# Mish as four nested products instead of five, in a fused attention and dense kernel whose softmax is shared by two engines

## The chip, the cores and the metric

The kernel runs on one core of a Trainium2 chip. A core has a matrix engine (TensorE, in the profile PE for matmuls and PEld for weight loads), a vector engine (VectorE, DVE), an engine for activation functions (ScalarE, ACT), a general one (GpSimd, POOL), and a queue that issues most transfers (SyncE, SP). They run at the same time and wait for each other by semaphores. The metric is the time of one execution on the device in microseconds, as the median of several runs; lower is better. Before the change it is 871.78 us (three runs, 871.4 to 873.9).

## The reference

Two branches over the same x (2048 tokens, 640 features, bf16), mixed by a gate per token. Branch A is attention with 32 heads of 20 dimensions; branch B is a dense layer to 1536 features, the Mish activation, and a dense layer back.

```python
qkv = (x @ wqkv).reshape(B, S, 3, H, Dh)            # H = 32, Dh = 20
scores = einsum("bhqd,bhkd->bhqk", q, k) * Dh ** -0.5
a = (softmax(scores) @ v) @ wo                      # heads put together first
h = x @ w1 + b1
sp = log1p(exp(-abs(h))) + where(h > 0, h, 0)       # softplus
b = (h * tanh(sp)) @ w2                             # Mish of h, then w2
g = sigmoid((x * gate_w).sum(-1, keepdims=True))
out = g * a + (1 - g) * b
```

## The kernel before

The kernel is written as a plan: Python code walks through the program in the order in which it should run, keeps an estimated clock for each engine, and appends each operation to its engine's list. The order on every engine is thus fixed when the kernel is built, and it depends on the planner's costs, due times and limits.

The backbone is the softmax. Its 2048 score tiles (128 keys by 512 queries, by head and block; the last block in two halves) are worked off in 683 slots of three tiles. In each slot TensorE makes three score tiles in one half of six PSUM banks (`emit_s`, L1062), ScalarE exponentiates them in one instruction into the tile ETS (`emit_e`, L1084), and TensorE multiplies the result with V (`pv`, L1198). Two slots of scores are in flight, five slots of ETS.

In some slots one tile, a "unit", is taken off ScalarE. ScalarE then exponentiates two tiles (1024 columns), and VectorE makes the exponential of the third from the bits of the number: one instruction that evicts the scores from PSUM with a scale and an offset (L1112), and three of 512 columns that correct it with a polynomial (two of L1128, one of L1130; `emit_x`). Two such chains, with the tiles EM and ER, run interleaved. `choose` decides for each slot whether it gives off a unit: only if a buffer is free, if VectorE's backlog is under BEHIND, and if a unit's chain (estimated by CHAIN) ends before its head group does. Before that, the condition in the main loop (L1519) allows no unit where tasks are late by LAG slots and the backlog is over SPARE, or where `room` finds that the VectorE work still owed (MISH per hidden task among it) does not fit the slots that are left.

Between slots TensorE is given tasks from a list by due time: the projections for Q, K and V, packed into shared tiles and moved through DRAM (QS, KS) by SP; the hidden layer `h_task` (L851, eviction with bias on VectorE, L861), the output of branch B `b_task` (L911, eviction times 1 - g in `OMG`, L918), and the output projection `p_task` (L935, mixing in L941). Matmuls without use (L1472, and repeated scores) fill TensorE's idle time. After each head group VectorE copies the accumulated output out (L1276) and divides it by the row sums, which go through three small transfers on SP's queue (RR, SUMS, BCT; L1279 to L1289).

The part that is changed belongs to branch B. Two `h_task`s fill 1024 columns of HB. Then `mish` appends one ScalarE instruction, a tanh of half the (shifted) h into the tile U, in W2R or REG (L884), and a chain of VectorE instructions of 1024 columns (L900 to L904), which leave the activation in HB. They wait in the lane `blend`, from which `work` picks them when VectorE's planned time has a hole. There are 24 such groups. The activation is left without its constant factor, which stands in `OMG` (L759) and is multiplied in with the gate. A test of the inputs' size (`flag_ops`, `flag_end`) must end before the first hidden task; it chooses between this program and a slower one that is not run here.

## Time and profile before

| | |
|---|---|
| median of three runs | 871.78 us (871.4 to 873.9) |
| the profiled execution | 871.46 us, of it the span 869.6 us |
| PE busy | 756.0 us (87%), 6350 matmuls |
| DVE busy | 827.8 us (95%), 1306 instructions |
| ACT busy | 852.5 us (98%), 714 instructions |
| transfers | 48.42 MB, 56 GB/s on average |
| exponentials (L1084) | 683, 833.9 us busy |
| tanh (L884) | 18 to REG, 23.0 us; 6 to W2R, 7.1 us |
| third-tile evictions (L1112) | 77 + 70 + 33 + 25 + 11 = 216 |

The span is what the profiler saw from the first instruction to the last; the execution's own time has some 2 us around it. Busy times are those of the recorded intervals. Records of neighbouring instructions on one engine overlap a little, so the mean duration of a record is longer than the step from one start to the next. A row of a group reads: line, engine, operation, tile written <- tiles read, shape, count, then busy time and mean ns of one, then the idle time of the engine before them and who ended it.

### The profile page before, as it was taken

The page shows a single profiled execution, that of the slowest core. Times are in us where ns is not written, and L with a number is a line of the kernel's source. Part 1 is how long each engine was busy: PE and PEld are TensorE (multiplying, and loading weights), DVE is VectorE, ACT ScalarE, POOL GpSimd, SP SyncE. Part 2 cuts the span into 40 slices and gives each one's busy share as a digit, 9 for nine tenths or more (in the row PEclk, how much of TensorE's full clock was granted, in tenths as well). Part 3 has the DMA queues.
Part 4 walks back from the last instruction along what each step waited for, and adds up shares of the span by engine and source line. Part 5 has one row for each costly group of instructions (what it writes and reads, how often), then busy time and mean ns, then how long its engine had stood idle before and what let it go on. Part 6 is the DMA issues. An engine that isn't in the chain of part 4 may idle for free.

```text
span 869.6 us, 15516 instructions
## 1 busy us (share of the span) xinstructions
PE 756.0 (87%) x6350; PEld 262.6 (30%) x6395; DVE 827.8 (95%) x1306; ACT 852.5 (98%) x714; POOL 7.3 (1%) x14
## 2 busy tenths in 40 slices
PE   7888888888889988899888898898888889889896
PEld 3333332233223332223223333232333233233232
DVE  5799999999999999999999999999999999999995
ACT  6999999999999999999999999999999999999996
POOL 2000000000000000000000000000000000000000
PEclk9999999999999999999999999999999999999998
DMA  9611310011233222302111121111212121010001
GB/s 223 86 60 40 108 40 24 11 59 49 76 90 99 64 59 71 122 16 49 32 44 44 59 60 47 47 32 56 60 43 69 48 60 52 8 29 26 18 14 35
DMA packets 76318, 48.42 MB, mean 56 GB/s; under 512 B 22104, under 2 KB 71888, under 8 KB 76192
## 3 DMA queue, kind: packets, MB, share of 16 engines
q1 hardware_dynamic: 73872, 46.86, 19.7%
q8 instruction: 53, 0.87, 0.4%
q10 hardware_dynamic: 2256, 0.47, 0.3%
q0 software_dynamic: 112, 0.01, 0.1%
q14 instruction: 25, 0.20, 0.1%
HBM read 37.64 MB, written 7.52 MB: 52 GB/s over the span
## 4 chain that ended last, share of the span: by engine, by line
ACT 93%; PE 3%; DVE 3%; DMA 1%; issue 0%; DVEq 0%; SPq 0%
ACT ETS L1084 90%; ACT REG L884 2%; PE PS L1062 1%; ACT W2R L884 1%; DMA OTN<-in_A_x_dram 1%; DMA RR<-OUNG 0%; PE PS L1198 0%; DVE ER L1128 0%; PE PS L607 0%; DVE EM L1128 0%; DVE HB L861 0%; PE PS L851 0%; PE PS L935 0%; PE PS L679 0%; DVE W2R L1112 0%
## 5 line engine op out<-in xcount | busy, mean ns | idle before, releaser
L1084 ACT ACTIVATE ETS<-PS 128x1536 bf16<-128x1536 f32 (+1 forms) x683 | 833.9, 1488 | 2.1 <-PE PS L1062 1.9
L1062 PE MATMUL PS<-QT,KT 32*128 32x512 bf16 (+1 forms) x2221 | 278.0, 378 | 93.8 <-ACT ETS L1084 78.9
L1198 PE MATMUL PS<-ETS,V_all 128*21 128x512 bf16 (+1 forms) x1888 | 211.7, 380 | 0.9 <-DVE OUNG L1276 0.4
L1062 PEld LDWEIGHTS PS<-QT,KT 32*128 32x128 bf16 x2221 | 69.1, 91 | 307.4 <-ACT ETS L1084 281.2
L1198 PEld LDWEIGHTS PS<-ETS,V_all 128*21 128x21 bf16 x1888 | 48.5, 89 | 95.2 <-issue 87.5
L911 PE MATMUL PS<-W2R,HB 128*128 128x320 bf16 x384 | 73.7, 302 | 0.3 <-DVE HB L861 0.2
L1128 DVE SCALAR_TENSOR_TENSOR ER<-ER 128x512 f32<-128x512 f32 x108 | 73.6, 681 | 0.1
L1128 DVE SCALAR_TENSOR_TENSOR EM<-EM 128x512 f32<-128x512 f32 x108 | 73.3, 679 | 0.1
L1112 DVE TENSOR_SCALAR REG<-PS 128x512 f32<-128x512 f32 x77 | 52.6, 685 | 3.9 <-PE PS L1062 2.5
L851 PE MATMUL PS<-XB,REG 128*128 128x256 bf16 x360 | 55.2, 275 | 0.7 <-DVE HB L861 0.5
L1112 DVE TENSOR_SCALAR XE<-PS 128x512 f32<-128x512 f32 x70 | 48.0, 686 | 5.3 <-PE PS L1062 4.4
L911 PEld LDWEIGHTS PS<-W2R,HB 128*128 128x128 bf16 x384 | 28.4, 97 | 38.6 <-issue 27.4
L1472 PE MATMUL PS<-KT 128*128 128x512 bf16 x120 | 36.5, 383 | 2.3 <-issue 1.7
L851 PEld LDWEIGHTS PS<-XB,REG 128*128 128x128 bf16 x360 | 27.9, 97 | 26.0 <-issue 23.9
L861 DVE TENSOR_TENSOR HB<-PS,B1T 128x512 bf16<-128x512 f32 x48 | 32.7, 682 | 0.3
L901 DVE SCALAR_TENSOR_TENSOR U<-U 128x1024 f32<-128x1024 f32 x24 | 29.1, 1213 | 0.0
L902 DVE SCALAR_TENSOR_TENSOR U<-U,HB 128x1024 f32<-128x1024 f32 x24 | 29.0, 1209 | 0.0
L1128 DVE SCALAR_TENSOR_TENSOR EM<-REG 128x512 f32<-128x512 uint16 x39 | 26.6, 683 | 0.3
L1130 DVE SCALAR_TENSOR_TENSOR REG<-EM,REG 128x512 int32<-128x512 f32 x39 | 26.5, 679 | 0.0
L1128 DVE SCALAR_TENSOR_TENSOR ER<-REG 128x512 f32<-128x512 uint16 x38 | 25.9, 683 | 0.2
L1130 DVE SCALAR_TENSOR_TENSOR REG<-ER,REG 128x512 int32<-128x512 f32 x38 | 25.8, 680 | 0.0
L935 PE MATMUL PS<-WOQ,QT 128*128 128x320 bf16 x128 | 25.1, 305 | 0.7 <-DVE HB L941 0.3
(136 smaller groups left out, 827.1 us busy)
## 6 DMA issues: line engine op xcount, KB each, us to landing
REG<-in_B_w_dram SPq DMA_DIRECT2D x36, 320.0 KB, 3.1
BCT<-SUMS SPq DMA_DIRECT2D x31, 256.0 KB
W2R<-in_B_w_dram SPq DMA_DIRECT2D x12, 320.0 KB, 3.2
KT<-KS SPq DMA_DIRECT2D x28, 128.0 KB
QT<-QS SPq DMA_DIRECT2D x112, 20.0 KB
QS<-WOQ SPq DMA_DIRECT2D x16, 128.0 KB, 2.1
KS<-OTN SPq DMA_DIRECT2D x16, 128.0 KB, 1.7
W2R<-in_B_w_dram SPq DMA_DIRECT2D x1, 1920.0 KB, 8.9
```

The costliest lines, as they stand in the source:

```text
L851: return lambda e, bank: e.matmul(PS[:, bank, i * HW:(i + 1) * HW], w1b(n1)[:, f, i * P:(i + 1) * P], xt(c)[:, f, cols], start=(f == 0), s ...
L861: ev = dve(lambda e: e.tensor_tensor(hb, PS[:, bank, :].rearrange("p (i t) -> p i t", i=2), bias, ALU.add), [last, b_load, *guarded, *b_re ...
L901: piece(two, lambda e: e.scalar_tensor_tensor(U2[:, :], U2[:, :], EVEN[0], U2[:, :], ALU.add, ALU.mult))
L902: piece(two, lambda e: e.scalar_tensor_tensor(U2[:, :], U2[:, :], EVEN[1], h, ALU.add, ALU.mult))
L911: return lambda e, bank: e.matmul(PS[:, bank, 0:HALF], HB[:, hc % 2, f, t * P:(t + 1) * P], W2[:, f, half * HALF:(half + 1) * HALF], start ...
L1062: op = pl.add("pe", lambda e, i=i, g=real(g), tile=tile, j=j, cols=cols, c=c, of_q=of_q: e.matmul(scores(s)[:, i, cols], KT[32 * j:32 * j ...
L1084: e_op[s] = pl.add("act", lambda e: e.activation(ETS[:, s % NETS, 0:n, :], scores(s)[:, 0:n, :], AF.Exp, scale=SCALE, bias=LIFT if fast el ...
L1112: ev_op[s] = dve(lambda e: e.tensor_scalar(y, scores(s)[:, 2, :], SCALE * ULPS, BIAS, ALU.mult, ALU.add), [s_op[s], ei_free[b], *(wkv_read ...
L1128: piece(WIDE, lambda e, v=m if i else f, i=i: e.scalar_tensor_tensor(m, v, STEPS[i], v, ALU.add, ALU.mult), lambda i=i: () if i else [lane ...
L1130: piece(WIDE, lambda e: e.scalar_tensor_tensor(x, m, LAST_STEP, y, ALU.mult, ALU.add))
L1198: lasts[n] = pl.add("pe", lambda e, tile=tile, h=real(g) * HG + j, j=j, src=src[:, cols], of_q=of_q, count=count: e.matmul(PS[32 * j:32 * ...
L1472: pl.add("pe", lambda e: e.matmul(PS[:, bank, :], k[:, 0:P], k, start=True, stop=True), [free], cost=PASS, kind="S")
```

## The change

Mish was computed from t = tanh(h/2 - ln(2)/4) by five VectorE instructions: t squared, that times (itself + a constant), times h with another constant added, times (t + 1), times (t - ZERO). Now t = tanh((h - MISH_AT)/2) with another shift, and the result is a polynomial of degree six in t times h, in four instructions that each add a constant to one operand and multiply by another: p = (t + c0) t; p = (p + c1) t; t = (p + c2) h, written over the tanh; h = (p + c3) t. The constant factor in `OMG` changes with it. Three of the planner's constants change as well: the time set aside for a unit's chain (CHAIN), for the Mish of a hidden task (MISH), and the lateness at which units are held back (LAG). Nothing else is edited; the order of the instructions is planned anew from these.

```diff
-CHAIN = 3.3
+CHAIN = 2.7
...
-MISH = 2.8
+MISH = 2.25
...
-LAG = 12
+LAG = 9
...
-ZERO = 3 + 2 * math.sqrt(2)
-EVEN = (-7.3284271269269485, 43.27570311039964)
-EVEN_BY = -0.002803081308334686
+MISH_STEPS = (1.5274980615848066, -5.90257334954394, 18.967422148121276, -6.430071830749512)
+MISH_BY = -0.006540836794009846
+MISH_AT = 0.6830045149697055
...
                 gate_done.append(dve(lambda e: e.tensor_scalar(
-                    OMG[:, :], GATE[:, :], -EVEN_BY, EVEN_BY, ALU.mult, ALU.add), [r]))
+                    OMG[:, :], GATE[:, :], -MISH_BY, MISH_BY, ALU.mult, ALU.add), [r]))
...
-                ex = pl.add("act", lambda e: e.activation(U, h, AF.Tanh, scale=0.5, bias=-math.log(2) / 4), [ev, u_free[0]], cost=0.95)
+                ex = pl.add("act", lambda e: e.activation(U, h, AF.Tanh, scale=0.5, bias=-MISH_AT / 2), [ev, u_free[0]], cost=0.95)
...
                 two = 2 * WIDE - 0.07
-                piece(two, lambda e: e.tensor_tensor(U2[:, :], U, U, ALU.mult))
-                piece(two, lambda e: e.scalar_tensor_tensor(U2[:, :], U2[:, :], EVEN[0], U2[:, :], ALU.add, ALU.mult))
-                piece(two, lambda e: e.scalar_tensor_tensor(U2[:, :], U2[:, :], EVEN[1], h, ALU.add, ALU.mult))
-                piece(two, lambda e: e.scalar_tensor_tensor(U2[:, :], U, 1.0, U2[:, :], ALU.add, ALU.mult))
-                piece(two, lambda e: e.scalar_tensor_tensor(h, U, -ZERO, U2[:, :], ALU.add, ALU.mult), done)
+                steps = ((U2[:, :], U, U), (U2[:, :], U2[:, :], U), (U, U2[:, :], h), (h, U2[:, :], U))
+                for n, (to, one, by) in enumerate(steps):
+                    piece(two, lambda e, n=n, to=to, one=one, by=by: e.scalar_tensor_tensor(
+                        to, one, MISH_STEPS[n], by, ALU.add, ALU.mult), done if n == 3 else None)
```

## The prediction

> **What bounds the kernel now.** I read the page first: the busy shares, the forty slices, the chain of waits, and the row of the exponentials.

> ```profile
> span 869.6 us, 15516 instructions
> ...
> DVE  5799999999999999999999999999999999999995
> ACT  6999999999999999999999999999999999999996
> ...
> ACT 93%; PE 3%; DVE 3%; DMA 1%; issue 0%; DVEq 0%; SPq 0%
> ...
> L1084 ACT ACTIVATE ETS<-PS 128x1536 bf16<-128x1536 f32 (+1 forms) x683 | 833.9, 1488 | 2.1 <-PE PS L1062 1.9
> ```

> ScalarE is the chain: 93% of it, and its 683 exponentials were preceded by 2.1 us of idle time in all. VectorE is nearly as full. The two share one job. A slot is three 128x512 score tiles; ScalarE exponentiates all three, or two, while VectorE makes the third with four instructions of its own. So VectorE time that comes free can be turned into shorter slots on ScalarE, and the price is the exchange rate between the two. For that I asked for ScalarE's groups with the shapes kept apart, over the whole run and over one stretch of 72 us without any other ScalarE work, the chain's piece for that stretch, and a run of ten triples near the end.

> ```profile
> L1084 ACT ACTIVATE ETS<-PS 128x1536 bf16<-128x1536 f32 x466 | 672.7, 1620 | 1.8 <-PE PS L1062 1.5
> L1084 ACT ACTIVATE ETS<-PS 128x1024 bf16<-128x1024 f32 x217 | 245.5, 1205 | 0.3 <-PE PS L1062 0.3
> ```

> ```profile
> L1084 ACT ACTIVATE ETS<-PS 128x1536 bf16<-128x1536 f32 x38 | 54.7, 1625 | 0.0
> L1084 ACT ACTIVATE ETS<-PS 128x1024 bf16<-128x1024 f32 x24 | 26.0, 1208 | 0.0
> ```

> ```profile
> 347.21 73.14 ACT ETS L1084 x62
> ```

> ```profile
> 843.19 13.53 ACT L1084 ACTIVATE ETS<-PS 128x1536 bf16<-128x1536 f32 x10
> ```

> Records of consecutive instructions overlap, so the durations (1620 and 1205 ns) are longer than the steps from one start to the next. Ten triples in a row take 13.53 us; less one record of 1.62 that is nine steps, 1.32 us each. In the 62-slot piece 38 triples are 50.2 us at that step, and the 24 pairs have the other 22.9 us: 0.955 us each. A pair therefore saves 1.32 - 0.955 = 0.37 us over a triple. The records alone give 1.620 - 1.205 = 0.415. The difference between the two is time in which the slot after a pair had to wait a little for its scores.

> What a VectorE instruction costs is read in the same way, from its timeline:

> ```profile
> 635.32 0.68 DVE L1128 SCALAR_TENSOR_TENSOR ER<-REG 128x512 f32<-128x512 uint16 x1
> 635.92 0.68 DVE L1128 SCALAR_TENSOR_TENSOR EM<-EM 128x512 f32<-128x512 f32 x1
> 636.52 0.68 DVE L1128 SCALAR_TENSOR_TENSOR ER<-ER 128x512 f32<-128x512 f32 x1
> 637.13 0.68 DVE L1244 TENSOR_TENSOR QT<-OUNG,BCT 128x512 bf16<-128x512 f32 x1
> 637.73 1.21 DVE L900 TENSOR_TENSOR U<-REG 128x1024 f32<-128x1024 f32 x1
> 638.87 0.68 DVE L1130 SCALAR_TENSOR_TENSOR REG<-EM,REG 128x512 int32<-128x512 f32 x1
> 639.47 0.54 DVE L918 TENSOR_SCALAR XB<-PS,OMG 128x320 bf16<-128x320 f32 x1
> 639.95 0.69 DVE L1112 TENSOR_SCALAR REG<-PS 128x512 f32<-128x512 f32 x1
> 640.55 1.22 DVE L901 SCALAR_TENSOR_TENSOR U<-U 128x1024 f32<-128x1024 f32 x1
> 641.69 0.69 DVE L1130 SCALAR_TENSOR_TENSOR REG<-ER,REG 128x512 int32<-128x512 f32 x1
> ```

> A 512-column instruction starts 0.60 us after the one before it, whichever of the four it is; a 1024-column one takes 1.14 us (637.73 to 638.87, and 640.55 to 641.69), the plain product of L900 no less than the three-operand form of L901.

> **The change, part by part.** *One product fewer.* Five 1024-column instructions per Mish become four, all of the three-operand form.

> ```profile
> L901 DVE SCALAR_TENSOR_TENSOR U<-U 128x1024 f32<-128x1024 f32 x24 | 29.1, 1213 | 0.0
> L902 DVE SCALAR_TENSOR_TENSOR U<-U,HB 128x1024 f32<-128x1024 f32 x24 | 29.0, 1209 | 0.0
> ```

> There are 24 of each, so 24 x 1.14 = 27.4 us leave VectorE. By itself that shortens nothing, because VectorE is not the chain. The first product is of the other form now and the third writes over the tanh; neither changes a price, as all forms above cost the same. The Mish's last result comes one instruction sooner, which nobody waits for visibly.

> *What the planner buys with it.* The instruction lists of the two built programs can be compared: VectorE's evictions of a third tile go from 216 to 228, ScalarE's two-tile exponentials from 217 to 229 (one is the last, short slot), and its 683 slots and 24 tanhs stay. On ScalarE this gives 12 x 0.37 = 4.4 us by the steps, 12 x 0.415 = 5.0 us by the records. I take 0.38, nearer the steps because they contain the waits: **-4.6 us**. On VectorE it costs 12 x 4 x 0.60 = 28.8 us. Net, VectorE has 28.8 - 27.4 = 1.4 us more to do in 4.6 us less time. That must come out of its idle time, so I compared the two orders by stretch of slots and asked for the busy time in the same stretches (25-200 is about slots 12-160, then 162-280, 280-400, 400-600, 600-670, and the end):

> ```profile
> 25.00:200.00 175.00, 152.37 (x1355) 53.91 (x1376) 167.10 (x282) 174.52 (x149) 0.00 (x0) 1.00 0.22 53
> 200.00:354.00 154.00, 135.73 (x1104) 46.67 (x1115) 149.07 (x236) 153.50 (x129) 0.00 (x0) 1.00 0.25 73
> 354.00:500.00 146.00, 128.41 (x1012) 41.20 (x1013) 143.35 (x230) 146.00 (x125) 0.00 (x0) 1.00 0.18 52
> 500.00:760.00 260.00, 227.60 (x1865) 80.38 (x1864) 257.30 (x372) 260.00 (x216) 0.00 (x0) 1.00 0.17 49
> 760.00:843.00 83.00, 74.01 (x624) 24.66 (x629) 80.89 (x136) 82.99 (x71) 0.00 (x0) 1.00 0.07 19
> 843.00:869.60 26.60, 17.71 (x224) 6.87 (x225) 15.77 (x31) 17.96 (x15) 0.86 (x1) 0.91 0.12 39
> ```

> After the window and its length, the pairs are busy time and count of PE, its weight loads, DVE, ACT and POOL, then the granted clock. Up to slot 162 (about 204 us) both programs are the same, 59 units each. Then, units before and after: 33 and 35 with six Mish; 44 and 46 with three; 53 and 58 with fifteen; 27 and 30 with none. With 2.40 us for a unit and 1.14 off each Mish, VectorE's load changes by -2.0, +1.4, -5.1 and +7.2 us in these four, while ScalarE's falls by 0.8, 0.8, 1.9 and 1.1. Only the last stretch gets tighter by much: 7.2 + 1.1 = 8.3 us, against 83.00 - 80.89 = 2.1 us of visible idle time and about 3 us that the stretch before it has to spare. Some room lies beyond it: VectorE is idle 26.60 - 15.77 = 10.8 us in the end part. I count no loss there, with up to 3 us in the range.

> *Moved work.* The first three Mish groups come earlier (their tanhs stand at slots 170 to 198, not 210 to 234), so the flag test, the w1 loads (320 KB each) and the hidden projections pass some packed Q/K moves on SP's queue. Behind those loads on SP stand the three small DMAs that normalize a head group, and VectorE's reciprocal waits for the first of these. What such waiting costs now:

> ```profile
> W2R<-in_B_w_dram SPq DMA_DIRECT2D x12, 320.0 KB, 3.2
> ```

> ```profile
> PE PS L1062 <- ACT ETS L1084: 78.9, 203, 1.2
> ...
> DVE RR L1283 <- DMA RR<-OUNG: 1.6, 2, 1.4
> ```

> (Of a wait: us in total, times, the longest.) Two waits, 1.6 us in all, in an engine that is not the chain. ScalarE would feel it only if several head groups were held up in a row; I price it between a gain of 0.5 us and a loss of 1.5 us, by that row, and take 0. The planner's three constants act through this order alone and have no cost besides.

> *PE.* The new order has 34 fewer filler matmuls (L1472, 137 to 103 issued) and 19 fewer score matmuls. PE waits 203 times for ScalarE before a score, at most 1.2 us, and is off the chain, so this is worth nothing.

> The sum, against the profiled execution's own 871.46 us (span 869.6, 1.86 around it; 0.32 below the median of 871.78): 871.46 - 4.6 = 866.9, and with a little of the 0.32 back, **867.0 us**.

> [...]

> **The rivals.** *VectorE sets the pace in the last stretch* (slots 600 to 682). If it has no room there, each late eviction holds up the scores two slots on, and the 8.3 us are paid by ScalarE: 871.46 - 4.6 + 8.3 = 875.2; with the visible 2.1 us of idle time used, 873.1. It decides against the change once the room there is under 8.3 - 4.6 = 3.7 us. For it: 2.1 us visible, and VectorE at 97% in this stretch. Against: gaps under the records' overlap of 0.08 are not seen as idle, the stretch before is relieved, and late in the run any backlog can run into the 10.8 us of the end part.

> *Half of it is lost in waits.* More pairs in a row leave PE less time per slot, and the denser stretches stall for part of the 3 us set aside above: about 870. For it: a pair already saves 0.04 us less than its records say. Against: ScalarE idles 2.1 us in the whole run.

> *The time stays.* The added pairs fall where something else sets the pace, or the reordered Q/K moves after slot 162 hold up a head group by as much as is gained: 871.5. For it: SP's queue is rearranged most there. Against: the 12 units are spread over all four stretches.

> *It gains more.* ScalarE gets the full 0.415, and the earlier Mish groups free another us by moving work from stretches without idle time: 865.4.

> *PE's clock drops* for lack of filler work: 3.4 us of half clock somewhere, up to 2 us lost, 869. The granted clock is 1.00 in every stretch but the end, and the longest wait above is 1.2 us. I fold it into the second rival.

> **How the numbers follow.** Forecast 867.0: 0.68, with its own range 865.6 to 868.8. Half lost, about 870: 0.15. VectorE in the last stretch, 873 to 875: 0.08. Time stays: 0.05. More gain: 0.04. The range takes the likeliest, the larger gain and most of the half-lost case: 865.2 to 870.9. A change of 0.3%, 2.6 us, is about what a measurement of this kernel can tell from none: faster is under 869.2, slower over 874.4. Faster: 0.68 + 0.04 + a fifth of the half-lost case, 0.75. Slower: most of the VectorE case, 0.06. Same: 0.19.

> **What would show it.** Right: 229 pairs and 454 triples with records near 1.2 and 1.62 us, ScalarE's idle time before exponentials still about 2 us, four Mish rows of 24 with 1.21 us records, VectorE's busy time up by 1 to 3 us, and the time from slot 162 on shorter by 4 to 5 us with the first 204 us unchanged. Wrong: idle time of ScalarE above 4 us; scores that wait for VectorE's L1112 instead of ScalarE, above all after 750 us (the last stretch); reciprocals waiting long for their DMA between 200 and 354 us (SP's queue); a granted clock below 1.00 before the end.

## The result, and the profile after

The changed kernel takes 867.3 us (median of five runs, 866.4 to 867.8) against 872.0 for the one before in the same session; the ratio is 0.9939, 95% interval 0.9923 to 0.9954. Measured again later, beside other kernels, it was 0.9924 (0.9911 to 0.9936). The kernel became faster by 0.6%, some 5 us; 4.8 were forecast. A profile shows one execution, and the ratios are those of the medians, so the two can differ by a few us.

The profiled execution took 866.43 us. From its page (lines of code have moved up by one, so L1083 is L1084 of before):

```profile
span 864.6 us, 15494 instructions
...
PE 756.3 (87%) x6342; PEld 259.5 (30%) x6342; DVE 829.4 (96%) x1330; ACT 847.8 (98%) x714; POOL 7.3 (1%) x14
...
DVE  4799999999999999999999999999999999999996
ACT  6999999999999999999999999999999999999996
...
ACT 94%; PE 4%; DMA 1%; DVE 0%; issue 0%; SPq 0%
```

ScalarE is the chain as before, now 94% of it, and its busy time fell by 4.7 us. VectorE has 24 more instructions and 1.6 us more busy time (827.8 to 829.4), in a span that is 5.0 us shorter. ScalarE's exponentials by shape, and the products of Mish where the tanh lies in REG (the other six groups have it in W2R):

```profile
L1083 ACT ACTIVATE ETS<-PS 128x1536 bf16<-128x1536 f32 x454 | 649.3, 1585 | 1.2 <-PE PS L1061 1.0
L1083 ACT ACTIVATE ETS<-PS 128x1024 bf16<-128x1024 f32 x229 | 252.5, 1181 | 0.7 <-PE PS L1061 0.7
```

```profile
L902 DVE SCALAR_TENSOR_TENSOR U<-REG 128x1024 f32<-128x1024 f32 x18 | 21.9, 1218 | 0.0
L902 DVE SCALAR_TENSOR_TENSOR U<-U,REG 128x1024 f32<-128x1024 f32 x18 | 21.9, 1217 | 0.0
L902 DVE SCALAR_TENSOR_TENSOR HB<-U,REG 128x1024 bf16<-128x1024 f32 x18 | 21.9, 1217 | 0.0
L902 DVE SCALAR_TENSOR_TENSOR REG<-U,HB 128x1024 f32<-128x1024 f32 x18 | 21.9, 1214 | 0.0
```

Twelve triples have become pairs, idle time before exponentials is 1.9 us in all (2.1 before), and a product of Mish costs what it did.

Where the 5 us came from is seen by counting the exponentials in ScalarE's timeline of both runs and taking the time from the start of one slot to the start of another (units are counted in the same trace, the forecast is that of the prediction):

```
slots           before us (units)   after us (units)   change    forecast
start to 0        10.02               10.33             +0.3       0
0 to 162         193.80 (59)         193.89 (59)        +0.1       0
162 to 280       150.76 (33)         149.35 (35)        -1.4      -0.8
280 to 400       145.21 (44)         145.35 (46)        +0.1      -0.8
400 to 600       260.63 (53)         258.04 (58)        -2.6      -1.9
600 to 682        99.31 (27)          97.85 (30)        -1.5      -1.1
682 to the end     9.88                9.75             -0.1       0
```

The stretch that gave nothing is 280 to 400. One place in it, slot 293, shows how a pair is spent without a gain; TensorE's and ScalarE's timeline there (start, length, instruction):

```profile
367.09 0.39 PE L1061 MATMUL PS<-QT,KT 32*128 32x512 bf16 x3
367.42 0.72 PE L910 MATMUL PS<-W2R,HB 128*128 128x320 bf16 x4
368.06 0.40 PE L1197 MATMUL PS<-XE,V_all 128*21 128x512 bf16 x1
368.07 0.41 PE L1197 MATMUL PS<-REG,V_all 128*21 128x512 bf16 x1
368.08 0.61 PE L1197 MATMUL PS<-ETS,V_all 128*21 128x512 bf16 x4
368.62 0.39 PE L1061 MATMUL PS<-QT,KT 32*128 32x512 bf16 x3
```

```profile
369.06 1.02 ACT L1083 ACTIVATE ETS<-PS 128x1024 bf16<-128x1024 f32 x1 [0.19 <-PE PS L1061]
```

From one group of scores to the next (367.09 to 368.62) it is 1.5 us, as the four matmuls of branch B and the six products with V, which stand between them in TensorE's list, ran in that order; the slot is a pair of 0.90. The next exponential starts 0.6 us late, and most of that hides behind the end of the last record: the view shows 0.19 us of idle time. In steps from one start to the next, an undisturbed triple takes 1.331 us in both runs and an undisturbed pair 0.904 (the medians). What the steps of slots 280 to 400 exceed these by rose from 1.4 to 2.4 us, of which slot 293 is 0.6. That ate the gain of these two units.

### The profile page after: what moved, and what is told of

It reads as the page before. It is cut to its first block, busy times and chain, and to the rows that moved or that the text cites. A ratio compares the mean times of both kernels' runs of the same rounds, so it can differ in the third digit from the quotient of the medians.

```text
span 864.6 us, 15494 instructions
## 1 busy us (share of the span) xinstructions
PE 756.3 (87%) x6342; PEld 259.5 (30%) x6342; DVE 829.4 (96%) x1330; ACT 847.8 (98%) x714; POOL 7.3 (1%) x14
## 2 busy tenths in 40 slices
ACT  6999999999999999999999999999999999999996
## 4 chain that ended last, share of the span: by engine, by line
ACT 94%; PE 4%; DMA 1%; DVE 0%; issue 0%; SPq 0%
ACT ETS L1083 92%; ACT REG L884 2%; PE PS L1061 1%; PE PS L1197 1%; ACT W2R L884 1%; DMA OTN<-in_A_x_dram 1%; PE PS L607 0%; PE PS L910 0%; PE PS L670 0%; DVE HB L940 0%; PE PS L774 0%; PE PS L679 0%; PE PS L851 0%; PE PS L541 0%; PE PS L1471 0%
## 5 line engine op out<-in xcount | busy, mean ns | idle before, releaser
L1083 ACT ACTIVATE ETS<-PS 128x1536 bf16<-128x1536 f32 (+1 forms) x683 | 827.6, 1449 | 1.9 <-PE PS L1061 1.7
L1127 DVE SCALAR_TENSOR_TENSOR ER<-ER 128x512 f32<-128x512 f32 x114 | 77.9, 683 | 0.1
L1127 DVE SCALAR_TENSOR_TENSOR EM<-EM 128x512 f32<-128x512 f32 x114 | 77.7, 682 | 0.0
L1111 DVE TENSOR_SCALAR REG<-PS 128x512 f32<-128x512 f32 x85 | 58.2, 685 | 1.9 <-PE PS L1061 1.0
L1111 DVE TENSOR_SCALAR XE<-PS 128x512 f32<-128x512 f32 x78 | 53.3, 686 | 5.3 <-PE PS L1061 4.3
L910 PEld LDWEIGHTS PS<-W2R,HB 128*128 128x128 bf16 x384 | 28.1, 97 | 38.6 <-issue 27.4
L851 PEld LDWEIGHTS PS<-XB,REG 128*128 128x128 bf16 x360 | 27.9, 97 | 29.1 <-issue 27.2
L1471 PE MATMUL PS<-KT 128*128 128x512 bf16 x103 | 32.0, 385 | 0.0
L1129 DVE SCALAR_TENSOR_TENSOR REG<-EM,REG 128x512 int32<-128x512 f32 x43 | 29.3, 681 | 0.0
L1127 DVE SCALAR_TENSOR_TENSOR EM<-XE 128x512 f32<-128x512 uint16 x39 | 26.8, 686 | 0.3
L1127 DVE SCALAR_TENSOR_TENSOR ER<-XE 128x512 f32<-128x512 uint16 x39 | 26.7, 686 | 0.3
L1129 DVE SCALAR_TENSOR_TENSOR XE<-EM,XE 128x512 int32<-128x512 f32 x39 | 26.6, 683 | 0.1
```

Source lines behind the costliest of these rows:

```text
L851: return lambda e, bank: e.matmul(PS[:, bank, i * HW:(i + 1) * HW], w1b(n1)[:, f, i * P:(i + 1) * P], xt(c)[:, f, cols], start=(f == 0), s ...
L910: return lambda e, bank: e.matmul(PS[:, bank, 0:HALF], HB[:, hc % 2, f, t * P:(t + 1) * P], W2[:, f, half * HALF:(half + 1) * HALF], start ...
L1083: e_op[s] = pl.add("act", lambda e: e.activation(ETS[:, s % NETS, 0:n, :], scores(s)[:, 0:n, :], AF.Exp, scale=SCALE, bias=LIFT if fast el ...
L1111: ev_op[s] = dve(lambda e: e.tensor_scalar(y, scores(s)[:, 2, :], SCALE * ULPS, BIAS, ALU.mult, ALU.add), [s_op[s], ei_free[b], *(wkv_read ...
L1127: piece(WIDE, lambda e, v=m if i else f, i=i: e.scalar_tensor_tensor(m, v, STEPS[i], v, ALU.add, ALU.mult), lambda i=i: () if i else [lane ...
L1129: piece(WIDE, lambda e: e.scalar_tensor_tensor(x, m, LAST_STEP, y, ALU.mult, ALU.add))
```

## The experiments

All kernels are compared with the kernel before by ratio; the times are medians. Units are counted from each kernel's instruction lists.

**The product without the units.** The slots and tiles to be given off come from a list, those of the kernel before; the rest is the changed kernel.

```diff
-            if (len(order) < SLOT or home() is None
-                    or late + urgent + other >= BEHIND):
+            u = GIVEN.get(s)
+            if u is None or home() is None:
                 return None
...
-                compose(step + 2, choose(step + 2) if fast and step >= CALM and (step < slot_of(0, 1, 0) or behind < CATCH_UP and (lag < LAG or backlog() < SPARE) and room()) else None)
+                compose(step + 2, choose(step + 2) if fast else None)
```

> Four products as in the changed kernel, but the units are given by a list: the slots and tiles that the kernel before gave to VectorE, of which 215 of 216 find a free buffer (13 fewer than the changed kernel's 228). VectorE keeps the 27 us of the fifth product as idle time. Theory (only the units that are bought shorten the run): no gain over before, 867.3 + 13 x 0.38 = 872.2, between 871 and 873.5. Rival (VectorE's lateness held ScalarE up before, so that free VectorE time helps by itself): 867 to 869.5.

874.0 us, ratio 1.0020 (1.0009 to 1.0031). Its page:

```profile
PE 760.6 (87%) x6379; PEld 261.5 (30%) x6379; DVE 803.7 (92%) x1278; ACT 853.0 (98%) x714; POOL 7.3 (1%) x14
```

VectorE has 24 us less to do than before and is idle for 8% of the span, and nothing is gained: ScalarE's 853.0 us are no less than the 852.5 of before. The rival falls: without the units the removed product buys nothing. The run is 0.2% slower than before, some 1.7 us, and its one unit fewer explains 0.4 of that; the rest comes with the given list.

**Fewer units.** The same, with the changed kernel's own list, about every ninth left out.

> Four products, the changed kernel's own list of units with about every ninth left out: 200 units. It measures the exchange rate. Theory, 0.38 us a unit net of waits: 867.3 + 28 x 0.38 = 877.9 (876.7 to 879.2). By the records alone, 0.415 a unit: 878.9. If the last units bought were worth little because the run is bound elsewhere by then: under 876.

879.5 us, ratio 1.0082 (1.0051 to 1.0114). Against the list of 215, 15 units are worth (1.0082 - 1.0020) x 872 = 5.4 us, 0.36 each. Against the changed kernel, 28 are worth (1.0082 - 0.9939) x 872 = 12.5 us, 0.45 each, and this comparison holds the cost of the list, too. With the intervals of the ratios the two are 0.36 give or take 0.2 and 0.45 give or take 0.1. The price of 0.38 lies between, but so does 0.415; these runs don't tell the two apart.

**More units without the time for them.** The kernel before, with a planned time for VectorE that is too short.

```diff
-WIDE = 0.60
+WIDE = 0.57
```

> Five products as before, with the planner's time for a 512-column VectorE instruction set from 0.60 to 0.57 us, so that it gives off 232 units, 16 more than before, without the VectorE time for them: 16 x 2.4 = 38 us more VectorE work and nothing removed. It tests where VectorE becomes the bound. Rival of the prediction (VectorE has no room): slower than before, 875 to 890, with scores waiting for VectorE's evictions. If VectorE had room for it: 872.0 - 16 x 0.38 = 865.9. I expect about 878.

894.1 us, ratio 1.0263 (1.0235 to 1.0291). ScalarE's exponentials and the waits for them:

```profile
L1084 ACT ACTIVATE ETS<-PS 128x1536 bf16<-128x1536 f32 x450 | 627.4, 1494 | 17.2 <-PE PS L1062 16.1
L1084 ACT ACTIVATE ETS<-PS 128x1024 bf16<-128x1024 f32 x233 | 239.8, 1080 | 6.5 <-PE PS L1062 5.7
```

```profile
PEld PS L911 <- DVE XB L918: 8.1, 10, 1.3
PE PS L851 <- DVE HB L861: 7.0, 11, 1.2
PEld PS L1198 <- DVE OUNG L1276: 5.2, 8, 1.6
```

ScalarE idles 23.7 us where it idled 2.1. The scores are late because TensorE stands in front of other matmuls, ahead of them in its list, whose bank VectorE has not emptied: its matmuls wait 54 us for VectorE, where they waited 10 before. The largest single loss is another: at slot 198 TensorE waits 3.8 us for a w1 load (W2R), and the exponential comes 4.7 us late. So the room for 38 us more is not there in this plan. That 28 us more, for 228 units, would not fit without the removed product is an inference. The edit also makes every planned VectorE time of this size 5% too short, so part of the loss can be a worse order; no run separates the two.

**The constants and the product apart.** The changed kernel with CHAIN, MISH and LAG of before, and the kernel before with those of the changed one (the three lines of the diff, one way and the other).

> Four products with the three planner constants of before (CHAIN 3.3, MISH 2.8, LAG 12): 227 units, one fewer than the changed kernel. It tests whether the product or the constants bring the gain. Theory (the product): 867.3 + 0.4 = 867.7, ratio to before about 0.995. Rival (the constants, through a better order): 870 or more.

869.1 us, ratio 0.9957 (0.9940 to 0.9974).

> Five products with the three constants of the changed kernel: 219 units, 3 more than before, with no VectorE time for them. The planner now counts less VectorE work than there is. Theory: 872.0 - 3 x 0.38 = 870.9 if the room is there, up to 873 if the 7 us of VectorE work lack it; ratio 0.998 to 1.002. Rival (the constants bring the gain): 868 or less.

876.7 us, ratio 1.0048 (1.0031 to 1.0065). The product brings most of the gain without the constants, and the constants without the product lose 0.5%, more than I expected: in that run three slots alone (196, 198 and 208) start 1.1, 1.5 and 0.8 us late. The first run's 1.8 parts in a thousand above the changed kernel are more than its one unit, but the intervals meet, so what the constants add to the product is not settled.

**No filler on TensorE.** A return at the head of `fill_up`.

> The changed kernel without any filler matmul (neither L1471 between slots nor repeated scores); 227 units. The prediction counted 34 fewer fillers as worth nothing because PE is off the chain. If the granted clock stays at 1.00: 867.3 + 0.4, within 866.5 to 869. If TensorE's clock falls in stretches: scores come late after pairs and the time is 870 or more, with a mean clock under 0.99.

883.1 us, ratio 1.0115 (1.0098 to 1.0131), mean granted clock 0.926. Windows of this kernel (length, then busy time and count of each engine, granted clock, DMA share, GB/s):

```profile
25.00:200.00 175.00, 151.41 (x1319) 53.08 (x1336) 163.50 (x273) 172.03 (x145) 0.00 (x0) 0.95 0.23 57
200.00:354.00 154.00, 130.60 (x1056) 42.91 (x1064) 150.31 (x242) 153.66 (x130) 0.00 (x0) 0.97 0.23 67
354.00:500.00 146.00, 127.39 (x916) 37.10 (x913) 137.45 (x225) 141.46 (x120) 0.00 (x0) 0.83 0.18 48
500.00:760.00 260.00, 226.69 (x1805) 79.85 (x1802) 254.67 (x380) 258.04 (x216) 0.00 (x0) 0.98 0.18 51
760.00:843.00 83.00, 73.45 (x535) 21.16 (x533) 78.69 (x131) 80.30 (x69) 0.00 (x0) 0.86 0.06 19
```

The time is lost where the clock is low. Slots 280 to 400 take 151.0 us here, 145.4 in the changed kernel. Over the whole run ScalarE's steps exceed their undisturbed lengths by 26.3 us, against 11.2 in the changed kernel. Of these 26.3, 16.9 lie in or just behind the pieces of half clock and 9.3 in all the rest. So the loss comes with the clock and not with the changed order.

**More units with the time for them.** Does VectorE have room for more than 228? Four edits of the planner gave off 231 to 234 units, one of them in two forms. First SLACK 0.5:

> The changed kernel with the planner's SLACK (how far a planned VectorE piece may run past the next due one) from 0.3 to 0.5 us, which gives 234 units, 6 more. VectorE gets 6 x 2.4 = 14 us more work. Theory, if the room is there: 867.3 - 6 x 0.38 = 865.0 (864 to 866.5). If VectorE sets the pace by now: 867.5 or more.

870.6 us, ratio 0.9972 (0.9955 to 0.9988): slower than the changed kernel. Its profile is of an execution of 868.1 us. There slots 162 to 280 and 280 to 400 take 149.3 and 143.6 us, as good as or better than in the changed kernel; slots 400 to 600 take 259.6 instead of 258.0, with 58 units in both, and slots 0 to 162, with 61 units, 195.7 instead of 193.9. Slot 34 alone starts 2.6 us late (ScalarE, then SP and TensorE):

```profile
54.34 3.28 ACT L1083 ACTIVATE ETS<-PS 128x1024 bf16<-128x1024 f32 x3 [2.38 <-PE PS L1061]
```

```profile
49.41 0.57 SPq L598 DMA_DIRECT2D KT<-KS  x1
...
53.90 0.61 PE L1061 MATMUL PS<-QT,KT 32*128 32x512 bf16 x6 [2.25 <-issue]
```

The row of TensorE names no releaser, but the trace tells what was late. The K load that SP issued at 49.41 us ended at 53.81; an instruction of TensorE's sequencer (L195) waited for its semaphore from 50.58 to 53.84, and the weights of these scores follow at 53.87. In the changed kernel the same wait lasts from 52.05 to 52.76, and slot 34 is not late.

Then I kept SLACK for the first 160 slots and gave the planner another time for a pair, 0.95 us. (That is about the mean step of a pair with its waits, 0.96; undisturbed it is 0.904.)

```diff
-EXP_PAIR = 0.908
+EXP_PAIR = 0.95
...
-            work(ready + (LATER if fast and now["rate"] < BUSY and now["bank"] else SLACK))
+            work(ready + (LATER if fast and now["rate"] < BUSY and now["bank"] else SLACK if now["step"] < 160 else 0.5))
```

> The changed kernel with two planner values edited: SLACK 0.5 instead of 0.3 from slot 160 on only, and the estimated time of a two-tile exponential at 0.95 us, what it measures, instead of 0.908. 233 units, 59 of them before slot 162 as in the changed kernel (the run with 234 had 61 there, and lost 2 us in that stretch). Theory: 867.3 - 5 x 0.38 = 865.4 (864.5 to 867). If VectorE has no room for 12 us more work: 867.5 or more.

872.8 us, ratio 0.9995 (0.9981 to 1.0010): no gain left. The new time for a pair changes the plan from the start, too: slots 0 to 162 take 195.5 us instead of 193.9, with the same 59 units. The largest single loss is at slot 198, in rows of SP, TensorE and ScalarE:

```profile
245.82 0.47 SPq L806 DMA_DIRECT2D W2R<-in_B_w_dram  x1
...
251.97 1.73 PE L851 MATMUL PS<-XB,W2R 128*128 128x256 bf16 x10 [3.88 <-DMA W2R<-in_B_w_dram]
...
253.64 0.61 PE L1061 MATMUL PS<-QT,KT 32*128 32x512 bf16 x3
...
254.29 4.29 ACT L1083 ACTIVATE ETS<-PS 128x1536 bf16<-128x1536 f32 x3 [4.00 <-PE PS L1061]
```

The w1 load that SP issued at 245.82 us, behind two K loads, landed at 251.93, 6.1 us later (the median of such loads is 3.2). TensorE waits 3.9 us for it with the scores queued behind, and ScalarE idles 4.0 us. It is the moved work of the prediction, with the price that it can have.

The same kernel with the load's landing planned at 3.2 us instead of 1.7 (its `tail`):

> The kernel with 233 units, with one more edit: the planner takes 3.2 us, what the trace shows, instead of 1.7 us from the end of a w1 load's issue to its landing, so that hidden projections are planned later behind their loads. 232 units. In the run with 233 units TensorE stood 3.9 us at a hidden projection whose w1 load was late behind Q/K moves on SP's queue, with scores queued behind it, and the exponential of slot 198 came 4.1 us late. Theory (that late load, not VectorE, spoiled the run): the wait for W2R is gone, and against the run with 233 the ratio falls from 0.9995 by 0.004 or more, to 0.992 to 0.996. Rival (VectorE has no room for more than 228): the ratio stays at 0.998 or more, with the loss spread over the stretches.

872.3 us, ratio 0.9987 (0.9976 to 0.9997). The wait for W2R is gone and slots 162 to 280 take 150.9 us instead of 153.1, but the ratio falls by 0.0008 where I had expected 0.004 or more, and it lies in the rival's range. That does not show the rival's reason, a VectorE without room. Slots 0 to 162 take 196.0 us here, 2.1 more than in the changed kernel with the same 59 units; slot 34, 1.3 us late, again starts its scores right behind a wait of TensorE's sequencer for that K load (50.27 to 52.42). The rest of the loss is in smaller waits.

With CROWD 1.3 as well, and EXP_PAIR as it was:

> The changed kernel with SLACK 0.5 from slot 160 on, CROWD 1.3 instead of 1.4, and the measured 3.2 us for w1 loads: 234 units, 59 before slot 162 and 62 in slots 400 to 600. Theory, with 6 x 0.38 = 2.3 us under the changed kernel: ratio 0.990 to 0.9935. If VectorE sets the pace: 0.995 or more, with ScalarE's idle time before exponentials above 4 us.

874.4 us, ratio 1.0012 (1.0000 to 1.0024), ScalarE idle 9.3 us, as the rival had it. Its first 162 slots are as short as the changed kernel's (193.4 us); slots 215, 409 and 410 start 2.2 to 2.5 us late, each behind products with V. And the changed kernel with CHAIN 2.2 alone:

> The changed kernel with CHAIN 2.2 instead of 2.7 and nothing else: 231 units, 3 more, with the first 162 slots at 59. Theory: 3 x 0.38 = 1.1 us under the changed kernel, ratio 0.991 to 0.994. If the unit's chain ends too late for its head group: the same or slower than the changed kernel.

877.2 us, ratio 1.0049 (1.0034 to 1.0064). Its profile, of a run of 873.3, shows a second kind of place, the end of a head group (VectorE, TensorE, ScalarE):

```profile
328.27 0.68 DVE L1129 SCALAR_TENSOR_TENSOR W2R<-ER,W2R 128x512 int32<-128x512 f32 x1
...
329.41 0.41 PE L1197 MATMUL PS<-W2R,V_all 128*21 128x512 bf16 x1
329.42 0.62 PE L1197 MATMUL PS<-ETS,V_all 128*21 128x512 bf16 x4
...
330.07 1.45 ACT L1083 ACTIVATE ETS<-PS 128x1536 bf16<-128x1536 f32 x1 [1.47 <-PE PS L1197]
```

A unit's last instruction comes when its group's other tiles are done; the products with V that finish the group wait for it, the ETS tiles stay full, and ScalarE has nowhere to write for 1.47 us. The slot after it is 1.9 us late too, again behind products with V. A smaller CHAIN lets the planner cut this closer; this is the condition that the expectation named, a chain that ends too late.

A part of what these kernels lose stands in no profile shown here. The nine executions with CHAIN 2.2 took 873.3 us (the profiled one, mean granted clock 0.998) to 879.8 (0.990), and the eleven of the last kernel with 234 units 871.0 (0.997) to 877.0 (0.986): by and large the longer, the lower the clock. All ten of the changed kernel had 0.998 or 0.999. In the profile of that last kernel TensorE is granted half its clock for 6.8 us from 517.3 us on, right after slot 409 was late, and slots 410 and 413 are late within that time. In the first kernel with 234 units the clock falls for 3.4 us at 54.8 us, right after the wait for the K load. A stall that starves TensorE thus seems to cost twice. More filler at these places was not tried.

**The changed kernel again**, as the yardstick on the same chip.

> The changed kernel itself, on the same chip as the three above, as their yardstick: ratio 0.9923 to 0.9954, as measured first.

866.6 us, ratio 0.9924 (0.9911 to 0.9936). None of the five kernels with more units beats it, and I have no version that does.

## Why the prediction was right

The likeliest case came in, 867.3 for 867.0, inside its own range. That the two are so close is in part luck: the profiled execution took 866.43 us where the sum gave 866.9, and the median lies 0.9 above that execution, where I had added 0.1. By its steps:

- *What bounds.* Right. VectorE's freed time alone gave nothing (the list of 215 units). ScalarE's shorter slots gave all: the steps of the 683 exponentials fell by 5.1 us, the span by 5.0.
- *One product fewer, -27.4 us of VectorE.* Right. The four products have the records of the five (1214 to 1218 ns, 1209 to 1216 before).
- *Twelve units at 0.38 us, -4.6.* A little small. From start to start the 683 exponentials of the two profiled runs sum to 830.4 and 825.3 us, a gain of 5.1. The undisturbed steps, 1.331 and 0.904, differ by 0.427, and twelve times that is 5.1, too; the records' 0.415 would have given 5.0. I had charged the added pairs with the waits of the old ones, but the waits over the whole run came to 14.0 us both times, as sums of steps over 1.331 and 0.904. That they did not grow is a balance, 1.0 more in slots 280 to 400 and as much less in the other stretches, which I had not foreseen. My reading of the steps was also a little off: I took the mean record, 1.62, for the last of the ten triples, which is 1.557 long, and so had 1.32 for 1.331. By the starts, the pairs of the 62-slot piece step by 0.934 and not 0.955, which makes 0.40 for a unit and 4.8 us for twelve.
- *VectorE's load, +1.4.* Measured +1.6 busy.
- *Moved work, 0.* Right for this order: the waits for RR (1.6 us) and W2R (0.5) of before are gone (VectorE idles 0.1 us in all before its 31 reciprocals), and slots 162 to 280 gained 0.6 more than their units. That the price cannot be large was wrong: I gave it 1.5 us as the worst, and the run with 233 units paid 4.1 at one slot for the same kind of move.
- *PE's filler, 0.* Right for 34 fewer, as the clock stayed at 1.00 up to the end part (0.98 there). The reason given, that PE is off the chain, was not enough: without any filler the run loses some 15 us against the changed kernel.

The rivals: VectorE did not set the pace in the last stretch; it is 1.5 us faster with its three units more, and these rows of the changed kernel show why there was room:

```profile
499.00:757.00 258.00, 224.88 (x1831) 78.74 (x1828) 254.83 (x380) 258.00 (x217) 0.00 (x0) 1.00 0.16 48
757.00:840.00 83.00, 76.06 (x640) 24.61 (x635) 81.78 (x140) 83.00 (x72) 0.00 (x0) 1.00 0.07 21
840.00:864.60 24.60, 15.93 (x208) 6.17 (x202) 17.71 (x35) 16.51 (x14) 0.86 (x1) 0.98 0.12 37
```

In the stretch itself busy time rose by 0.9 us (80.89 to 81.78 of 83), and in the end part by 1.9: 17.71 us in 24.60, where it was 15.77 in 26.60. That is less than half of the 7.2 that I had added there. The stretch before fell by 2.5 (257.30 to 254.83) where I had -5.1, so the work lies otherwise over the stretches than I took it to; the three together rose by 0.4. The half-lost case happened in one stretch, 280 to 400, by the way it named (TensorE has less time in a pair's slot), and was made up by the others.

What stays open: whether 228 is the most that this plan can hold. The edits that gave 231 to 234 moved everything behind them, and each met one or a few stalls of 1 to 4 us. Those that I followed are of two kinds: a load on SP's queue that lands late (K at slot 34, w1 at slot 198), and the last instruction of a unit that holds up the end of its head group. In the second it is VectorE that is late, so the rival that VectorE has no room for more than 228 is not ruled out. How much of the loss is the fall of TensorE's clock behind such stalls was not measured apart.

## What to carry to other kernels

Where two engines share a job, time saved on the one that is not the chain is worth its exchange rate: here 2.4 us of VectorE for 0.4 us of ScalarE, so 27 us removed gave 5. It gives nothing until the plan spends it, so count in the built program how many units it buys, and where. Beyond a point, spending more is paid at single places (a head group's end, a load behind other transfers, TensorE's order after a short slot). VectorE's busy share does not show that point: it is 96 to 97% in the five kernels with more units and 96% in the changed one. So a plan with more units must be measured.

## What the runs showed of the hardware

What went with the falls is how little streamed. In the trace without filler, back-to-back matmuls of 512 columns start 215 ns apart and those of 256 columns 108 ns, 0.42 ns a column. Counting each matmul, or group of concurrent ones, as its columns at that rate, the stretches of 3.4 us (as long as the shortest pieces) ahead of a fall held 24 to 41% of streaming; stretches that kept the full clock held 40% at the least and 60% in the median. In the other profiles the two ranges overlap between 38 and 46%, so this is no sharp limit (a few records are missing: without filler the page has 6119 matmuls for 6150 weight loads). That the little streaming lowers the clock is my inference from these counts; the run without filler (mean clock 0.926, in the changed kernel 0.999) agrees with it, and no run varied the streaming in steps.

By the profile's busy share the stretches ahead of a fall were busy for 37 to 65%, where 88% is the median. Such a share alone does not tell a fall either: in the kernel before TensorE was busy for 2.15 us of the 3.42 ahead of the piece at 854.53, and for 2.21 of 3.40 from 322.90 us on, where the clock stayed at 1.00. The share of a long stretch hides the falls: it is 87% where the clock was worst (127.39 of 146.00 us, clock 0.83), because matmuls at half clock took longer and count as busy. In the piece at 854.53 groups of 256-column score matmuls start 213 ns apart (120 just before it), and TensorE is busy for all of its 3.41 us.
